# Transposing queries and keys in 32x32 blocks on VectorE instead of TensorE, in a fused attention and expert-layer kernel

## The chip, the cores and the metric

The kernel runs on one core of a Trainium2 chip. The metric is the device time of one execution in microseconds (us). In the profile the engines are PE (TensorE matmul), PEld (TensorE weight load), DVE (VectorE), ACT (ScalarE), POOL (GpSimd) and SP (SyncE, which issues DMAs); "L412" is line 412 of the kernel file.

## The reference

Attention over 8 batches, 8 heads, 576 positions and a head width of 64, causal by blocks of 64 positions; then a layer with a softmax-gated activation and a normalization on the 4608 tokens.

```python
scores = scale * np.matmul(q, k.transpose(0, 1, 3, 2))       # scale = 1/8
scores = np.where(block_i >= block_j, scores, -1e9)          # blocks of 64
attn = np.exp(scores - max); attn = attn / (sum + 1e-09)
x = np.matmul(attn, v)            # heads side by side: x is [4608, 512]

h = x @ w_in                      # w_in [512, 1024]
sm = softmax(h); solu = h * sm
ln = (solu - mean) / np.sqrt(var + 1e-06) * g_ln
out = ln @ w_out                  # w_out [1024, 512]
```

q, k and v come as float32; w_in, w_out and g_ln are drawn with float64 words, and the kernel turns the weights' 64-bit words into float32 on the chip.

## The kernel before

**Work units.** There are 32 pairs (a batch and two of its heads) of attention and 36 tiles of 128 tokens for the expert layer ("moe" in the code). Four pairs give one batch of 576 tokens. The attention output of a batch stands in `xt`, which has three buffers; the third is also scratch space for preparing the weights (line 329), so the attention of batch 2 cannot write it before the weights are ready.

**Precision by two words.** Products that need more than TensorE's fast fp32r form are split: a value is converted to a high part and the low part is the difference (`qh`, `ql`, `kh`, `kl`, the weights' `wih`, `wil`, `woh`, `wol`, and the tiles' `xh`, `xl`, `ch`, `cl`). Three matmuls make one product: high x high, low x high, high x low.

**One pair, before** (lines 386 to 546). SP loads queries and keys with the positions on the partitions: `qr` holds four blocks of 128 positions, both heads side by side; `kr` holds the four blocks of keys and a fifth block, with the last 64 keys in its upper half and the last 64 queries in its lower half (lines 391 to 408). The runs in memory are 64 floats, 256 bytes. TensorE transposes the nine blocks against an identity matrix into PSUM (`trans`, lines 410 to 412, called at 419 and 420). ScalarE converts the PSUM results to the high parts (helper `copy`, line 384), VectorE subtracts for the low parts (L424, L425), and two small copies (ScalarE) and two small subtractions (VectorE, L429) put the last 64 queries of the two heads into the block-diagonal tiles `qdh` and `qdl`. The score matmuls (L445, and L439 for the last block) read these. Then come masks (L464), row maxima (L468, VectorE), exponentials (L472, ScalarE), reciprocals (L480, L481), the scaling of the probabilities (L488 on GpSimd, or L489 on VectorE), transposes of the probabilities (L499), and the product with v (L532). Queries' and keys' split tiles have two buffers, by even and odd pairs; `qr` and `kr` have one each.

**One tile of the expert layer** (lines 549 to 643). High and low parts of x (L564 or L572, L568), 24 matmuls with w_in (L589), maximum, exponential, product, centring, square, eight transposes (L624), their split (L628, L629), 24 matmuls with w_out (L637), the scaled copy to `ob` (L641) and the store (L643).

**Preparing the weights** (`prep`, lines 333 to 355, 16 pieces of 128x512). SP loads the raw words (L337) into `ub`; ScalarE turns the low words into integers (L339); VectorE clamps the high words (L340); a scaling down runs on ScalarE, GpSimd or VectorE (L341 to L343); VectorE shifts and joins (L344, L345) and adds the low words (L346); the pieces of w_out are multiplied by g (L349 ScalarE or L350 VectorE); the high part is converted (L351 or L352) and the low part subtracted (L353 VectorE or L354 GpSimd).

**What sets the order.** Every step is an `Op` with an engine, a planned duration in ns, a key, and the buffers that it reads and writes. `Schedule.run` (lines 101 to 192) simulates the five engines with these durations when the kernel is built: when an engine is free, it takes the ready operation with the smallest key, TensorE only if PSUM slots are free, and VectorE's operations that are marked `port` never in the same planned time as an operation of GpSimd. The order that comes out is the order of the instructions on the chip; the chip's own times are then ruled by semaphores. The keys are the pair's number, or `NP + h0 + done * hs` for tile `done`, plus a number for each kind of step out of `PARAMS`. An operation may have alternatives on other engines, with a penalty that is added to its key; an alternative with a penalty of 3 or more is not admitted (line 71). Names that end in "32" are for the first four pairs. `SWITCH` is the planned cost when TensorE goes over to another kind of operand layout (`mode`).

**PSUM.** Two slots of two banks ("D") and four of one bank ("S"). Before the change the transposed keys take a D slot and the transposed queries an S slot.

Of the kernel before, what the change touches and what calls it, by code (L numbers as in the profile page):

```python
# [195 lines left out]
def kernel(  # L196
# [136 lines left out]
    def prep(i, src, hi, lo, gcol, name, key):  # L333
# [6 lines left out]
        op("DVE", 335, lambda: DVE.tensor_scalar(out=T2, in0=high, scalar1=TOP, scalar2=-TOP, op0=ALU.min, op1=ALU.max), r=[kr_], w=[k2], key=key, port=True)  # L340
# [46 lines left out]
    def attention(p):  # L387
# [5 lines left out]
        for nm, src, dst, dk in (("qr", q, qr, K["ld" + sfx]), ("kr", k, kr, K["ld" + sfx]), (f"vr{i}", v, vt, K["lv" + sfx])):  # L393

            def load(nm=nm[:2], src=src, dst=dst, dma=ACT if p == 0 and nm == "kr" else SP):
                for h in range(2):
                    dma.dma_start(
                        dst[:, 0:4, 64 * h : 64 * h + 64],
                        src[b0, 2 * hp + h, 0:512, :].rearrange("(c p) d -> p c d", p=P),
                    )  # L400
# [7 lines left out]
            op("SP", {"qr": 1460, "kr": 1820, "vr": 1640}[nm[:2]], load, w=[nm], key=(K["l0"] if p == 0 else p) + dk, tail=2100)

        def trans(src, ps, n_):  # L410
            for c in range(n_):
                PE.transpose(PS(ps)[:, c * P : (c + 1) * P], src[:, c, :], ident)  # L412


        pq, pk = newps("S"), newps("D")
# [7 lines left out]
        copy(0, 512, lambda: (qh_, PS(pq)[:, 0:512]), 0.125, [("qh", i)], ke, pq)
        op("DVE", t_dve(S), lambda: DVE.tensor_tensor(out=kl_, in0=PS(pk)[:, 0:S], in1=kh_.bitcast(F32), op=ALU.subtract), r=[("kh", i)], w=[("kl", i)], key=ke, ps=pk)  # L424
        op("DVE", t_dve(512), lambda: DVE.scalar_tensor_tensor(out=ql_, in0=PS(pq)[:, 0:512], scalar=0.125, in1=qh_.bitcast(F32), op0=ALU.mult, op1=ALU.subtract), r=[("qh", i)], w=[("ql", i)], key=ke, ps=pq)  # L425
        for h in range(2):
            own, c_ = half[h], slice(64 * h, 64 * h + 64)
            copy(0, 64, lambda own=own, c_=c_: (qdh_[own, c_], PS(pk)[own, S : S + 64]), 0.125, [("qdh", i, h)], ke, pk)
            op("DVE", t_dve(64), lambda own=own, c_=c_: DVE.scalar_tensor_tensor(out=qdl_[own, c_], in0=PS(pk)[own, S : S + 64], scalar=0.125, in1=qdh_[own, c_].bitcast(F32), op0=ALU.mult, op1=ALU.subtract), r=[("qdh", i, h)], w=[("qdl", i, h)], key=ke, ps=pk)  # L429
# [258 lines left out]
```

## Time and profile before

| | |
|---|---|
| median of 3 runs | 811.03 us (810.62 to 813.65) |
| the profiled execution | 810.45 us, its span 808.7 us |
| mean granted TensorE clock | 0.985 |
| transposes of keys, queries on TensorE (L412) | 160 and 128 instructions |
| DMA | 123798 packets, 47.06 MB; 117072 packets under 512 bytes |
| loads of q, k and v | 128 KB: median 2.4 to 2.6 us from issue to landing; 32 KB: 2.2 to 2.4 us |
| loads of weights | 512 KB: 4.2 us (w_in), 3.5 us (w_out) |

A row of a group gives line, engine, operation, output <- inputs, shapes and count, then the busy time in us and the mean of one in ns, then the engine's idle time just before these instructions and what ended it. A row of the timeline gives start and length in us and how many instructions in a row were merged. TensorE's matmuls are pipelined, their ends are modelled, and a matmul's length overlaps with the next; from start to start is what it holds the engine.

### The profile page before, as it was taken

The page shows a single profiled execution, that of the slowest core. Times are in us where ns is not written, and L with a number is a line of the kernel's source. Part 1 is how long each engine was busy: PE and PEld are TensorE (multiplying, and loading weights), DVE is VectorE, ACT ScalarE, POOL GpSimd, SP SyncE. Part 2 cuts the span into 40 slices and gives each one's busy share as a digit, 9 for nine tenths or more (in the row PEclk, how much of TensorE's full clock was granted, in tenths as well). Part 3 has the DMA queues.
Part 4 walks back from the last instruction along what each step waited for, and adds up shares of the span by engine and source line. Part 5 has one row for each costly group of instructions (what it writes and reads, how often), then busy time and mean ns, then how long its engine had stood idle before and what let it go on. Part 6 is the DMA issues. An engine that isn't in the chain of part 4 may idle for free.

```text
span 808.7 us, 14263 instructions
## 1 busy us (share of the span) xinstructions
PE 785.2 (97%) x4975; PEld 623.2 (77%) x4975; DVE 464.5 (57%) x1248; ACT 536.5 (66%) x1414; POOL 238.4 (29%) x407
## 2 busy tenths in 40 slices
PE   7788899999999999999999999999999999999998
PEld 6656678777887877777878877777778787788886
DVE  4999997555455655544555455555445554344352
ACT  5998887667566766767766676776676666433243
POOL 2323643242323332223333333222333334011100
PEclk8989999999999999999999999999999999999999
DMA  7546421112221221122212222112221100000011
GB/s 168 150 119 165 128 62 30 51 45 59 58 58 45 58 58 45 42 57 58 58 44 58 45 58 58 43 50 51 58 58 51 50 19 12 27 22 18 13 40 39
DMA packets 123798, 47.06 MB, mean 58 GB/s; under 512 B 117072, under 2 KB 117072, under 8 KB 123728
## 3 DMA queue, kind: packets, MB, share of 16 engines
q1 hardware_dynamic: 122672, 45.90, 21.7%
q8 instruction: 39, 0.64, 0.3%
q10 hardware_dynamic: 1056, 0.26, 0.2%
q14 instruction: 31, 0.25, 0.1%
HBM read 36.70 MB, written 9.44 MB: 57 GB/s over the span
## 4 chain that ended last, share of the span: by engine, by line
PE 86%; ACT 5%; DVE 5%; issue 2%; POOL 1%; SPq 1%; DMA 1%; DVEq 0%; POOLq 0%
PE ps L589 25%; PE ps L637 23%; PE ps L499 10%; PE ps L532 9%; PE ps L445 8%; PE ps L624 5%; PE ps L412 3%; PE ps L439 3%; ACT pb L472 2%; DVE nm L468 1%; ACT xt L384 1%; POOL pb L488 1%; ACT pt L384 1%; DMA ub<-in_moe_w_in_dram 1%; PE ps L281 0%
## 5 line engine op out<-in xcount | busy, mean ns | idle before, releaser
L488 POOL TENSOR_SCALAR pb<-pb,rz 128x512 f32<-128x512 f32 (+4 forms) x267 | 150.7, 585 | 241.0 <-DVE rz L481 203.7
L472 ACT ACTIVATE pb<-ps,nm 128x384 f32<-128x384 f32 (+4 forms) x288 | 155.5, 548 | 68.7 <-DVE nm L468 68.6
L468 DVE TENSOR_REDUCE nm<-ps 128x1 f32<-128x384 f32 (+4 forms) x288 | 132.1, 505 | 53.3 <-PE ps L439 53.0
L384 ACT ACTIVATE pt<-ps 128x512 f32<-128x512 f32 (+1 forms) x224 | 113.6, 556 | 48.5 <-PE ps L499 47.6
L499 PE MATMUL ps<-ident,pb 128*128 128x128 f32 x800 | 111.0, 281 | 10.1 <-ACT pb L472 7.3
L499 PEld LDWEIGHTS ps<-ident,pb 128*128 128x128 f32 x800 | 93.2, 144 | 24.8 <-ACT pb L472 8.9
L612 POOL TENSOR_TENSOR ms<-ms,mhalf 128x1 f32<-128x1 f32 x36 | 19.9, 554 | 261.2 <-DVE ms L609 261.2
L532 PE MATMUL ps<-pt,vr 128*64 128x320 f32 (+4 forms) x896 | 93.6, 360 | 0.0
L629 DVE TENSOR_TENSOR cl<-ps,ch 128x512 fp32r<-128x512 f32 x72 | 47.7, 687 | 75.1 <-ACT ch L628 74.6
L589 PE MATMUL ps<-wih,xh 128*128 128x512 f32 x288 | 85.0, 417 | 0.0
L532 PEld LDWEIGHTS ps<-pt,vr 128*64 128x64 f32 x896 | 59.5, 137 | 32.9 <-issue 0.7
L637 PE MATMUL ps<-woh,ch 128*128 128x512 f32 x288 | 84.0, 413 | 0.0
L589 PE MATMUL ps<-wil,xh 128*128 128x512 f32 x288 | 78.9, 396 | 0.0
L637 PE MATMUL ps<-wol,ch 128*128 128x512 f32 x288 | 78.9, 395 | 0.0
L637 PE MATMUL ps<-woh,cl 128*128 128x512 f32 x288 | 78.6, 394 | 0.0
L589 PE MATMUL ps<-wih,xl 128*128 128x512 f32 x288 | 78.3, 393 | 0.0
L598 DVE TENSOR_SCALAR ms<-ms 128x1 f32<-128x1 f32 x36 | 5.5, 153 | 108.2 <-ACT ob L641 108.2
L641 ACT ACTIVATE ob<-ps,ms 128x512 f32<-128x512 f32 x36 | 24.8, 688 | 60.0 <-PE ps L637 55.1
L589 PEld LDWEIGHTS ps<-wil,xh 128*128 128x128 f32 x288 | 54.3, 188 | 12.8
L637 PEld LDWEIGHTS ps<-wol,ch 128*128 128x128 f32 x288 | 54.2, 188 | 12.8
L637 PEld LDWEIGHTS ps<-woh,cl 128*128 128x128 f32 x288 | 54.1, 188 | 12.9
L589 PEld LDWEIGHTS ps<-wih,xl 128*128 128x128 f32 x288 | 54.1, 188 | 12.6
(82 smaller groups left out, 1302.0 us busy)
## 6 DMA issues: line engine op xcount, KB each, us to landing
out_dram<-ob SPq DMA_DIRECT2D x36, 256.0 KB, 2.0
qr<-in_q_dram SPq DMA_DIRECT2D x64, 128.0 KB, 2.5
vr<-in_v_dram SPq DMA_DIRECT2D x64, 128.0 KB, 2.4
kr<-in_k_dram SPq DMA_DIRECT2D x62, 128.0 KB, 2.6
ub<-in_moe_w_in_dram SPq DMA_DIRECT2D x8, 512.0 KB, 4.2
ub<-in_moe_w_out_dram SPq DMA_DIRECT2D x8, 512.0 KB, 3.5
kr<-in_k_dram SPq DMA_DIRECT2D x32, 32.0 KB, 2.3
kr<-in_q_dram SPq DMA_DIRECT2D x32, 32.0 KB, 2.2
```

Source lines behind the costliest of these rows:

```text
L384: op("ACT", t_act(n_), lambda: ACT.activation(aps()[0], aps()[1], AF.Copy, scale=scale), r=r, w=w, key=key, ps=ps, alts=[("DVE", t_dve(n_) ...
L445: PE.matmul(PS(sps[h])[:, off : off + 128 * (i_ + 1)], w_[half[h], 128 * i_ : 128 * i_ + 128], x_[half[h], 0 : 128 * (i_ + 1)], start=n_ = ...
L468: op("DVE", t_dve(wid[u]), lambda sp=sp, off=off, u=u: DVE.tensor_reduce(out=nm_[u], in_=PS(sp)[:, off : off + wid[u]], axis=AX.X, op=ALU. ...
L472: op("ACT", t_act(wid[u], 186), lambda sp=sp, off=off, u=u, zg=zg, zc=zc: ACT.activation(pb[:, poff[u] : poff[u] + wid[u]], PS(sp)[:, off ...
L488: op("POOL", 0.836 * nn + 243, lambda b=b, nn=nn, zg=zg, zc=zc: POOL.tensor_scalar(out=pb[:, poff[b] : poff[b] + nn], in0=pb[:, poff[b] : ...
L499: PE.transpose(t[:, (s_ - c0) * P : (s_ - c0 + 1) * P], pb[:, poff[b] + j * P : poff[b] + (j + 1) * P], ident)
L532: PE.matmul(PS(avs[ph])[half[h], 64 * o_ : 64 * (o_ + n_)], vt[:, j, 64 * h : 64 * h + 64], pt_.rearrange("p s q -> p (s q)")[:, 128 * s_ ...
L589: PE.matmul(o_, a_[:, c, :], w_[:, c, s_], start=(si == 0 and c == 0), stop=(si == 2 and c == NKI - 1))
L624: PE.transpose(t_[:, c * P : (c + 1) * P], u[:, (4 * hf + c) * P : (4 * hf + c + 1) * P], ident)
L629: op("DVE", t_dve(512), lambda cs=cs, cps=cps: DVE.tensor_tensor(out=cl[:, cs, :].rearrange("p c q -> p (c q)"), in0=PS(cps), in1=ch[:, cs ...
L637: PE.matmul(o_, a_[:, c, :], w_[:, c, :], start=(hf == 0 and si == 0 and c == 0), stop=(hf == 1 and si == 2 and c == 7))
L641: op("ACT", t_act(512, 93), lambda: ACT.activation(ob[i], PS(ops_)[:, 0:DM], AF.Copy, scale=m[:, 3:4]), r=[("m3", i)], w=[("ob", i)], key= ...
```

## The change

**Loads.** Instead of `qr` and `kr`, each pair loads `qz` and `kz` [128, 576]. Four DMAs for each: DMA g fills partitions 32g to 32g + 31 with head g // 2 and columns 32 (g % 2) to 32 (g % 2) + 31 of its 64, as 18 blocks of 32 positions side by side. The runs in memory are 32 floats, 128 bytes. For the first pair the keys' four DMAs are issued by ScalarE's queue, all others by SP. The loads of v stay.

**Transposes.** VectorE transposes each 32x32 block of `kz` and `qz` within its place (two instructions of 128x576), which gives `kt` and `qt`: head and column on the partitions, position along the row, in SBUF. TensorE's transposes and their two PSUM slots are gone.

**Splits.** ScalarE, or GpSimd by an alternative, converts `kt` and `qt` to the high parts; VectorE subtracts for the low parts, now from SBUF. The keys' subtraction may also go to GpSimd if its penalty is admitted (a_kl is 129.132, so it is not). Queries are split over all 576 positions, and the last 64 go into `qdh` and `qdl` by four small copies on GpSimd; the two copies and two subtractions from PSUM are gone.

**Weights.** The clamp, the low words and the g scale get GpSimd as an alternative (the penalty of the low words, a_t3, is 111.852, so that one is not admitted; those of the clamp, -246.845, and of the g scale, -26.262, are).

**The plan.** `SWITCH` goes from 130 to 165; a planned 120 ns (`SLACK`) is added before a PSUM slot counts as free; the planned length of 12 matmuls goes from 12 x 231.5 to 12 x 233 ns; and all numbers in `PARAMS` are others, so the order of the whole program is planned anew.

```diff
-SWITCH = 130.0
+SWITCH = 165.0
+SLACK = 120.0
...
-    "nd": 2, "ld": 18.299, "lv": 3.426, "q": 15.658, "qe": 164.691, "s": -4.256, "se": -95.989,
+    "nd": 2, "ld": -112.86, "lv": 9.571, "q": 88.586, "qe": 132.144, "s": 58.329, "se": -84.684,
...
-    "h0": 143.478, "hs": 1.593, "h": -14.76, "he": 13.349, "c": 136.065, "sq": -88.891, "ct": -107.468,
+    "h0": 193.882, "hs": 32.26, "h": 3.059, "he": 101.927, "c": 19.936, "sq": -24.214, "ct": -56.228,
...
-    "e1": 248.397, "e2": 84.748, "a_sp": 15.65, "a_sp32": -32.586, "a_lf": -56.56, "a_w": 0.642,
+    "e1": 312.118, "e2": 188.943, "a_sp": 284.421, "a_sp32": 90.642, "a_lf": -193.984, "a_w": -185.932,
...
-                            heapq.heappush(events, (t + LAT[o.eng]["PE"], n, 3, x, None))
+                            heapq.heappush(events, (t + LAT[o.eng]["PE"] + SLACK, n, 3, x, None))
...
-    qr = sb("qr", [4, P])
-    kr = sb("kr", [5, P])
+    qz, kz, qt, kt = (sb(x, [S]) for x in ("qz", "kz", "qt", "kt"))
...
-        op("DVE", 335, lambda: DVE.tensor_scalar(out=T2, in0=high, scalar1=TOP, scalar2=-TOP, op0=ALU.min, op1=ALU.max), r=[kr_], w=[k2], key=key, port=True)
+        op("DVE", 335, lambda: DVE.tensor_scalar(out=T2, in0=high, scalar1=TOP, scalar2=-TOP, op0=ALU.min, op1=ALU.max), r=[kr_], w=[k2], key=key, port=True,
+           alts=[("POOL", 640, lambda: POOL.tensor_scalar(out=T2, in0=high, scalar1=TOP, scalar2=-TOP, op0=ALU.min, op1=ALU.max), K["a_cm"])])
...
+        for nm, src, dst in (("kz", k, kz), ("qz", q, qz)):
+
+            def load(nm=nm, src=src, dst=dst):
+                for g in range(4):
+                    dma = ACT if p == 0 and nm == "kz" else SP
                     dma.dma_start(
-                        dst[:, 0:4, 64 * h : 64 * h + 64],
-                        src[b0, 2 * hp + h, 0:512, :].rearrange("(c p) d -> p c d", p=P),
+                        dst[32 * g : 32 * g + 32, :].rearrange("p (g d) -> p g d", d=32),
+                        src[b0, 2 * hp + g // 2, :, 32 * (g % 2) : 32 * (g % 2) + 32].rearrange("(g p) d -> p g d", p=32),
                     )
...
-        op("PE", 109 * 5, lambda: trans(kr, pk, 5), r=["kr"], w=["k2"], key=kk, opens=pk)
-        op("PE", 109 * 4, lambda: trans(qr, pq, 4), r=["qr"], w=["q2"], key=kk, opens=pq)
...
+            op("DVE", t_dve(S), lambda z=z, t=t: DVE.transpose(t, z), r=[x + "z"], w=[x + "t"], key=kk)
+            op("ACT", t_act(S), lambda t=t, hi=hi, scale=scale: ACT.activation(hi, t, AF.Copy, scale=scale), r=[x + "t"], w=[(x + "h", i)], key=ke,
+               alts=[("POOL", 0.836 * S + 243, lambda t=t, hi=hi, scale=scale: POOL.tensor_scalar(out=hi, in0=t, scalar1=scale, scalar2=1.0, op0=ALU.mult, op1=ALU.mult), K["a_qh"])])
...
+                op("DVE", t_dve(S), lambda: DVE.tensor_tensor(out=kl_, in0=kt, in1=kh_.bitcast(F32), op=ALU.subtract), r=["kt", ("kh", i)], w=[("kl", i)], key=ke, port=True,
...
+        for x, dst, src in (("qh", qdh_, qh_), ("ql", qdl_, ql_)):
+            op("POOL", 300, lambda dst=dst, src=src: last(dst, src), r=[(x, i)], w=[(x + "d", i)], key=ke)
```

More of the change, by code (lines that the diff above doesn't have):

```diff
@@ L338, in prep @@
         high = raw[:, :, 1].bitcast(F32)
-        op("ACT", 520, lambda: ACT.activation(T3.bitcast(I32), raw[:, :, 0], AF.Copy, scale=2.0**-29), r=[kr_], w=[k3], key=key)
-        op("DVE", 335, lambda: DVE.tensor_scalar(out=T2, in0=high, scalar1=TOP, scalar2=-TOP, op0=ALU.min, op1=ALU.max), r=[kr_], w=[k2], key=key, port=True)
+        op("ACT", 520, lambda: ACT.activation(T3.bitcast(I32), raw[:, :, 0], AF.Copy, scale=2.0**-29), r=[kr_], w=[k3], key=key,
+           alts=[("POOL", 640, lambda: POOL.tensor_scalar(out=T3.bitcast(I32), in0=raw[:, :, 0], scalar1=2.0**-29, scalar2=1.0, op0=ALU.mult, op1=ALU.mult), K["a_t3"])])
+        op("DVE", 335, lambda: DVE.tensor_scalar(out=T2, in0=high, scalar1=TOP, scalar2=-TOP, op0=ALU.min, op1=ALU.max), r=[kr_], w=[k2], key=key, port=True,
+           alts=[("POOL", 640, lambda: POOL.tensor_scalar(out=T2, in0=high, scalar1=TOP, scalar2=-TOP, op0=ALU.min, op1=ALU.max), K["a_cm"])])
         op("ACT", 520, lambda: ACT.activation(T2, T2, AF.Copy, scale=DOWN), r=[k2], w=[k2], key=key,
@@ L392, in attention @@
         nm_, z_, rz_ = nmt[i], zt[i], rzt[i]
-        for nm, src, dst, dk in (("qr", q, qr, K["ld" + sfx]), ("kr", k, kr, K["ld" + sfx]), (f"vr{i}", v, vt, K["lv" + sfx])):
-            def load(nm=nm[:2], src=src, dst=dst, dma=ACT if p == 0 and nm == "kr" else SP):
-                for h in range(2):
+        half = [slice(0, 64), slice(64, 128)]
+        for nm, src, dst in (("kz", k, kz), ("qz", q, qz)):
+            def load(nm=nm, src=src, dst=dst):
+                for g in range(4):
+                    dma = ACT if p == 0 and nm == "kz" else SP
@@ L408, in attention @@
[L408 to L415, printed above, removed]
+                        dst[32 * g : 32 * g + 32, :].rearrange("p (g d) -> p g d", d=32),
+                        src[b0, 2 * hp + g // 2, :, 32 * (g % 2) : 32 * (g % 2) + 32].rearrange("(g p) d -> p g d", p=32),
+                    )
@@ new lines, in attention, with loadv @@
+            op("SP", 1600, load, w=[nm], key=(K["l0"] if p == 0 else p) + K["ld" + sfx], tail=2400)
+        def loadv():
+            for h in range(2):
+                SP.dma_start(
+                    vt[:, 0:4, 64 * h : 64 * h + 64],
+                    v[b0, 2 * hp + h, 0:512, :].rearrange("(c p) d -> p c d", p=P),
+                )
+            SP.dma_start(
+                vt[0:64, 4, :].rearrange("p (h d) -> p h d", h=2),
+                v[b0, 2 * hp : 2 * hp + 2, 512:576, :].rearrange("h p d -> p h d"),
+            )
@@ L423, in attention @@
[L423 to L429, printed above, removed]
+        for x, z, t, hi, lo, scale in (("k", kz, kt, kh_, kl_, 1.0), ("q", qz, qt, qh_, ql_, 0.125)):
+            op("DVE", t_dve(S), lambda z=z, t=t: DVE.transpose(t, z), r=[x + "z"], w=[x + "t"], key=kk)
+            op("ACT", t_act(S), lambda t=t, hi=hi, scale=scale: ACT.activation(hi, t, AF.Copy, scale=scale), r=[x + "t"], w=[(x + "h", i)], key=ke,
+               alts=[("POOL", 0.836 * S + 243, lambda t=t, hi=hi, scale=scale: POOL.tensor_scalar(out=hi, in0=t, scalar1=scale, scalar2=1.0, op0=ALU.mult, op1=ALU.mult), K["a_qh"])])
+            if x == "q":
+                op("DVE", t_dve(S), lambda: DVE.scalar_tensor_tensor(out=ql_, in0=qt, scalar=0.125, in1=qh_.bitcast(F32), op0=ALU.mult, op1=ALU.subtract), r=["qt", ("qh", i)], w=[("ql", i)], key=ke, port=True)
+            else:
+                op("DVE", t_dve(S), lambda: DVE.tensor_tensor(out=kl_, in0=kt, in1=kh_.bitcast(F32), op=ALU.subtract), r=["kt", ("kh", i)], w=[("kl", i)], key=ke, port=True,
+                   alts=[("POOL", 1380, lambda: POOL.tensor_tensor(out=kl_, in0=kt, in1=kh_.bitcast(F32), op=ALU.subtract), K["a_kl"])])
@@ L431, in attention, with last @@
+        def last(dst, src):
+            for h in range(2):
+                POOL.tensor_copy(dst[half[h], 64 * h : 64 * h + 64], src[half[h], 512:576].bitcast(F32))
+        for x, dst, src in (("qh", qdh_, qh_), ("ql", qdl_, ql_)):
+            op("POOL", 300, lambda dst=dst, src=src: last(dst, src), r=[(x, i)], w=[(x + "d", i)], key=ke)
         for g, (kind, us, masks) in enumerate(groups):
@@ L448, in attention @@
                 d, md = 3 * (t_mm(320) + t_mm(256)), 0
-                rd = [(x, i) for x in ("kh", "kl")] + [(x, i, h) for h in range(2) for x in ("qdh", "qdl")]
+                rd = [(x, i) for x in ("kh", "kl", "qhd", "qld")]
                 tiles = [(sps[0], [(LAST, 192)])]
@@ L454, in attention @@
                 tiles = [(sps[h], [((h, i_), off) for i_, off in us]) for h in range(2)]
-            op("PE", d, scores, r=rd + ["q2", "k2"], w=[("P2", i, u) for _, t in tiles for u, _ in t], key=p + K["s" + sfx], opens=tuple(sps), mode=md)
+            op("PE", d, scores, r=rd, w=[("P2", i, u) for _, t in tiles for u, _ in t], key=p + K["s" + sfx], opens=tuple(sps), mode=md)
             for sp, us_ in tiles:
```

23 lines of the change are left out of this document (9 added, 14 removed), and 8 rows, old and new, of the table PARAMS.

## Prediction

> **What bounds the kernel now.** I read first the page's busy shares and the chain that ended last, then a table of stages, then the order of TensorE's work in one steady cycle.
>
> ```profile
> span 808.7 us, 14263 instructions
> PE 785.2 (97%) x4975; PEld 623.2 (77%) x4975; DVE 464.5 (57%) x1248; ACT 536.5 (66%) x1414; POOL 238.4 (29%) x407
> PE ps L589 25%; PE ps L637 23%; PE ps L499 10%; PE ps L532 9%; PE ps L445 8%; PE ps L624 5%; PE ps L412 3%; PE ps L439 3%; ACT pb L472 2%; DVE nm L468 1%; ACT xt L384 1%; POOL pb L488 1%; ACT pt L384 1%; DMA ub<-in_moe_w_in_dram 1%; PE ps L281 0%
> ```
>
> TensorE is busy 97% of the span, and the transposes that the change removes (L412) are 3% of the chain. The stages, with busy time of PE, PEld, DVE, ACT and POOL, the granted clock, the DMA share and GB/s:
>
> ```profile
> 0.00:20.00 20.00, 15.58 (x82) 12.36 (x83) 9.65 (x31) 10.82 (x31) 5.08 (x24) 0.82 0.71 169
> 20.00:110.00 90.00, 77.11 (x527) 59.05 (x527) 87.24 (x226) 79.52 (x221) 33.16 (x37) 0.91 0.48 133
> 110.00:130.00 20.00, 18.69 (x132) 14.57 (x130) 16.94 (x42) 17.48 (x42) 11.71 (x17) 1.00 0.20 46
> 130.00:700.00 570.00, 568.94 (x3751) 451.94 (x3750) 306.76 (x858) 389.37 (x1053) 174.92 (x305) 1.00 0.19 49
> 700.00:809.00 109.00, 104.85 (x492) 85.26 (x490) 43.89 (x94) 39.29 (x70) 13.53 (x26) 1.00 0.07 27
> ```
>
> There are two regimes. From 130 us on TensorE is the bound: 568.94 of 570 us busy, VectorE 54%, ScalarE 68%. From 20 to 110 us, where the weights are prepared beside the first pairs, VectorE is the bound: 87.24 of 90 us (97%), ScalarE 88%, and TensorE has gaps and a clock of 0.91. Before 130 us TensorE lacks 130 - (15.58 + 77.11 + 18.69) = 18.6 us; afterwards 1.1 and 4.2 us. So the same removed instruction is worth its full time after 130 us and nothing by itself before.
>
> **What a removed transpose is worth.** Starts on TensorE in a steady cycle, and the transposes that begin between 100 and 700 us:
>
> ```profile
> 297.17 0.71 PE L412 MATMUL ps<-ident,kr 128*128 128x128 f32 x5
> 297.71 0.60 PE L412 MATMUL ps<-ident,qr 128*128 128x128 f32 x4
> 298.07 1.18 PE L637 MATMUL ps<-woh,ch 128*128 128x512 f32 x4
> ...
> 319.50 0.71 PE L412 MATMUL ps<-ident,kr 128*128 128x128 f32 x5
> ...
> L412 PE MATMUL ps<-ident,kr x125: 271/272/332, 116.0 to 655.7; 128*128 128x128 f32 x125
> ```
>
> The means of the instructions overlap, so I go by starts: nine transposes hold the engine from 297.17 to 298.07, 0.90 us, in a cycle of 22.33 us (297.17 to 319.50). What follows, L637, starts at once, so 0.90 us is what the cycle loses. 125 / 5 = 25 pairs transpose after 100 us, the first of them at 116; 24 lie in the TensorE-bound stage. Term one: 24 x 0.90 = **-21.6 us**. The other 8 pairs' 7.2 us lie in the stage that VectorE binds and only turn into idle time.
>
> What takes over after the removal: in 130:700, per pair of 23.75 us, ScalarE works 16.2 us and VectorE 12.8 us. VectorE gets about 1.1 us more (below), ScalarE a little less; both fit in a cycle of 21.4 us. The new chain load, VectorE transpose, conversion, subtraction is longer than the old one, but the operands have two buffers and no longer need PSUM, so it can run a pair ahead. I take it as hidden there by the 21 us of other work per pair; without that cover it would cost its two transposes and two subtractions, some 3 us a pair by the rows below.
>
> **What VectorE gains and loses in the first 130 us.**
>
> ```profile
> L468 DVE TENSOR_REDUCE nm<-ps 128x1 f32<-128x576 f32 x32 | 24.0, 750 | 53.1 <-PE ps L439 53.0
> L424 DVE TENSOR_TENSOR kl<-ps,kh 128x576 fp32r<-128x576 f32 x32 | 24.1, 754 | 8.5 <-ACT kh L384 7.8 <-ACT qdh L384 0.7
> L425 DVE SCALAR_TENSOR_TENSOR ql<-ps,qh 128x512 fp32r<-128x512 f32 x32 | 21.8, 681 | 6.8 <-ACT qh L384 6.8
> L429 DVE SCALAR_TENSOR_TENSOR qdl<-ps,qdh 64x64 fp32r<-64x64 f32 x64 | 14.1, 220 | 0.6
> L384 ACT ACTIVATE qdh<-ps 64x64 fp32r<-64x64 f32 x64 | 13.9, 217 | 7.5 <-DVE kl L424 7.0
> L352 DVE CAST woh<-xt 128x512 fp32r<-128x512 f32 x3 | 1.2, 412 | 0.0
> L568 POOL TENSOR_TENSOR xl<-xt,xh 128x512 fp32r<-128x512 f32 x32 | 41.2, 1287 | 21.6 <-PE ps L589 20.3 <-DVE xh L572 1.3
> L340 DVE TENSOR_SCALAR xt<-ub 128x512 f32<-128x512 f32 x16 | 6.8, 426 | 0.0
> L489 DVE TENSOR_SCALAR pb<-pb,rz 128x384 f32<-128x384 f32 (+4 forms) x21 | 7.5, 416 | 0.1
> L488 POOL TENSOR_SCALAR pb<-pb,rz 128x512 f32<-128x512 f32 x61 | 43.4, 724 | 18.2 <-DVE rz L481 9.0 <-ACT kh L384 3.1 <-ACT pt L384 2.9
> ```
>
> No VectorE transpose is in this trace. Its bounds for 128x576 fp32: as fast as the cast, 0.412 x 576/512 = 0.46 us, or as slow as GpSimd's two-input pass, 1.287 x 576/512 = 1.45 us. I take 0.75 us, as the two 128x576 rows that pass one element after the other (0.750 and 0.754). Per pair: two transposes +1.50; queries' low part over 576 columns instead of 512 +0.09; the two small subtractions for the last block (L429) -0.44. Net +1.15 us, for 8 pairs **+9.2 us**. Out go the weights' clamp, 16 x 0.426 = 6.8 us, if the planner gives it to GpSimd, and the 7.5 us of softmax scaling on VectorE (L489): the penalty a_sp32 goes from -32.6 to 90.6, and an alternative is only admitted under 3, so these 21 go to GpSimd for certain. VectorE's account: 9.2 - 14.3 = **-5.1 us**. With a transpose of 0.46 us it is -9.7; with 1.45 us +6.1; with no clamp moved +1.7.
>
> GpSimd had 38 of the first 110 us busy (5.08 + 33.16). It gains at 0.72 us each (the 128x512 row) 16 clamps and 21 scalings, 27 us, and the small copies for the last block: about 65 of 110, so it is not the bound. ScalarE loses two 0.22 us copies a pair and can hand the g scale over; it does not bind later than VectorE.
>
> The GpSimd work has another price, the way VectorE and GpSimd get at SBUF:
>
> ```profile
> 78.83 1.27 POOL L568 TENSOR_TENSOR xl<-xt,xh 128x512 fp32r<-128x512 f32 x1
> 78.84 0.68 DVE L425 SCALAR_TENSOR_TENSOR ql<-ps,qh 128x512 fp32r<-128x512 f32 x1
> 79.44 0.69 DVE L480 TENSOR_SCALAR z<-z 128x3 f32<-128x3 f32 x1
> ...
> L480 DVE TENSOR_SCALAR z<-z x64: 153/172/991, 15.0 to 679.0; 128x6 f32<-128x6 f32 x32, 128x3 f32<-128x3 f32 x32
> ```
>
> While GpSimd's pass ran until 80.10, the subtraction that reads PSUM kept its usual 0.68 us, but the small SBUF-only operation took 0.69 us instead of 0.17 (median) and ended as GpSimd did. After the change both subtractions read SBUF alone. In the first 130 us that is 16 operations; with GpSimd busy 37% (33.16 of 90) and a wait of half a 0.72 us operation, 16 x 0.37 x 0.36 = **+2 us**. In the TensorE-bound stage the same waits lie under TensorE's work.
>
> **The loads.** Rows of 256 bytes become 128 bytes for queries and keys: 2304 packets a pair become 4608. In 130:700 the 16 DMA engines were busy 0.19 x 16 x 570 / 24 = 72 us per pair; put wholly on the 3456 small packets of q, k and v that is at most 21 ns each. If a half-size packet costs as much, a pair's queries and keys take 4608 x 21 / 16 = 6.0 us instead of 3.0. In the steady stage the DMA share goes from 0.19 to about 0.33; nothing waits. Between 0 and 110 us it goes from 0.52 to about 0.74; the loads there are asked for a pair ahead, so I cost that at nothing. Only the very first pair has no cover: at most +3.0 us, at least 0; I take **+2 us**, since the keys' chain can start while the queries still arrive. The SP queue gets 11 issues a pair instead of 9, about 0.5 us each in 21 us:
>
> ```profile
> L397 SPq DMA_DIRECT2D qr<-in_q_dram x36: 497/518/817, 209.0 to 591.8; - x36
> ```
>
> The Trainium skill, page "DMA: Bandwidth & Descriptors", section "Why small descriptors are slow (HBM only)", gives each packet a fixed three cycles beside one cycle per 32 bytes. By it, as an estimate, a 128-byte packet costs 7 cycles against 11, the first pair loses 0.8 us instead of 3.0, and the sum below is some 1 us lower. No run here has such packets yet.
>
> **The sum.** First 130 us: -5.1 + 2 + 2 = -1.1 us. Against the profiled execution: 810.45 (1.75 of it outside the span) - 21.6 - 1.1 = 787.8 us; the median of the runs, 811.03, lies 0.6 above the profiled one, so 788.
>
> **Rivals.** First the forecast itself, 788: its own range is 780 to 794, from the transpose at 0.46 us (783) to no clamp moved (794).
>
> *GpSimd blocks VectorE in the weights' stage.* Five operations of each of the 16 weight pieces and the 16 subtractions, 96 in all, use SBUF alone on VectorE. If GpSimd's share there rises from 0.37 to 0.60, 80 x 0.23 x 0.36 + 16 x 0.60 x 0.36 = 10 us are lost instead of 2: 796, and 802 with a slower transpose. For it: the 79.44 row. Against it: the plan already keeps such operations apart. The Trainium skill says this as a rule, page "SBUF — State Buffer", section "SBUF: two separate sides": VectorE and GpSimd share one pair of ports, held for a whole instruction, also by a VectorE operation with two SBUF inputs. The 79.44 row agrees.
>
> *The gaps of the first stage fill.* More freedom for the weights' steps takes VectorE and ScalarE off the end of that stage, and of TensorE's 18.6 us of gaps before 130 us only some 6 stay: 788 - 12.6 = 775.
>
> *Attention runs ahead of the expert tiles* (the slower side). The tiles' key rises by 32.26 per tile instead of 1.593, while a pair's rises by 1. What attention alone and tiles alone cost:
>
> ```profile
> 29.80 0.77 PE L412 MATMUL ps<-ident,kr 128*128 128x128 f32 x5
> ...
> 43.78 0.77 PE L412 MATMUL ps<-ident,kr 128*128 128x128 f32 x5
> ...
> 702.10 11.16 PE ps L589 x48
> 726.16 11.16 PE ps L589 x48
> ```
>
> A pair with no tile beside it takes 13.98 us (29.80 to 43.78); a tile alone 12.03 us (two in 702.10 to 726.16). Together 26.0 us against 22.33 mixed: each pair that comes apart loses 3.7 us and its 0.90 us gain. Five such pairs eat the 22.7 us; twelve of 24 give 788 + 12 x 4.6 = 843. Against it: the attention output has three buffers, so attention cannot lead far, and TensorE takes any ready work.
>
> *The cycle does not shorten.* Another engine turns out to hold the 22.33 us, and only the small first-stage terms change: about 809. Against it: 99.8% TensorE with ScalarE at 68%.
>
> **Chances and range.** Forecast 0.66, blocked ports 0.15, filled gaps 0.10, attention ahead 0.05, cycle unchanged 0.04. One measurement of this kernel tells about 0.5% (4 us) from no change, so below 807 is faster: 0.66 + 0.15 + 0.10 = 0.91; within 0.5%: 0.04; slower: 0.05. The range 775 to 800 takes in the filled gaps and most of the blocked ports and leaves out the last two.
>
> **What would show it.** L412 gone; the steady cycle near 21.4 us with TensorE still above 99% busy from about 130 us; VectorE transposes near 0.75 us; the weights' clamp and all softmax scaling on GpSimd; TensorE's lack before 130 us near 25 us, since its removed work turns into idle time there. Wrong would be: a steady TensorE share under 97%, a transpose over 1.5 us, VectorE operations stretched beside GpSimd, or weights ready later than the last prepared piece is now.

## The result and the profile after

| | before | after |
|---|---|---|
| median | 812.34 us (4 runs, 810.62 to 814.20) | 790.44 us (4 runs, 788.92 to 791.23) |
| ratio, 95% interval | | 0.9728 (0.9697 to 0.9758) |
| profiled execution, its span | 810.45 us, 808.7 us | 790.35 us, 788.6 us |
| TensorE busy, and the rest of the span | 785.2 us, 23.5 us | 760.3 us, 28.3 us |

The forecast was 788 us in a range of 775 to 800. The page after, first its head, then its busy shares and the chain that ended last:

```profile
span 788.6 us, 13834 instructions
PE 760.3 (96%) x4687; PEld 595.4 (76%) x4687; DVE 471.7 (60%) x1191; ACT 521.6 (66%) x1349; POOL 341.7 (43%) x593
PE ps L650 25%; PE ps L602 25%; PE ps L512 10%; PE ps L545 9%; PE ps L458 8%; PE ps L637 4%; PE ps L452 3%; ACT pb L485 2%; DVE nm L481 1%; DMA ub<-in_moe_w_out_dram 1%; DMA kz<-in_k_dram 1%; DMA ub<-in_moe_w_in_dram 1%; POOL pb L501 0%; ACT xt L389 0%; DVE ql L432 0%
```

TensorE has 288 instructions less, and its transposes of queries and keys, 3% of the chain before, have no successor there. GpSimd went from 238.4 to 341.7 us. (Lines have moved: scores are L458 and L452 now, the transposes of probabilities L512, the product with v L545, the expert matmuls L602 and L650.) The stages after, with the same columns as before (PE, PEld, DVE, ACT, POOL, clock, DMA share, GB/s):

```profile
0.00:20.00 20.00, 9.70 (x46) 7.66 (x46) 11.78 (x30) 10.59 (x27) 8.57 (x29) 0.81 0.91 184
20.00:110.00 90.00, 78.31 (x522) 58.74 (x524) 81.97 (x200) 77.58 (x216) 62.77 (x99) 0.85 0.62 130
110.00:130.00 20.00, 18.03 (x129) 13.17 (x123) 18.10 (x45) 16.55 (x45) 12.42 (x20) 1.00 0.48 113
130.00:700.00 570.00, 569.52 (x3602) 447.31 (x3603) 325.42 (x847) 384.83 (x1013) 247.54 (x431) 1.00 0.22 47
700.00:789.00 89.00, 84.75 (x395) 68.53 (x393) 34.39 (x72) 32.06 (x54) 10.39 (x18) 0.99 0.07 27
```

The two regimes stand as before: TensorE 99.9% busy from 130 to 700 us, and a first stage in which it has gaps, now 130 - (9.70 + 78.31 + 18.03) = 24.0 us against 18.6. The steady cycle in TensorE's order of time, one matmul group and the same group a cycle later:

```profile
299.20 1.10 PE L602 MATMUL ps<-wil,xh 128*128 128x512 f32 x4
...
320.65 1.10 PE L602 MATMUL ps<-wil,xh 128*128 128x512 f32 x4
```

21.45 us against 22.33: 0.88 us less per pair. What the new operations cost, in the groups of VectorE and GpSimd:

```profile
L434 DVE TENSOR_TENSOR kl<-kt,kh 128x576 fp32r<-128x576 f32 x32 | 25.9, 809 | 1.3 <-ACT kh L429 1.3
L432 DVE SCALAR_TENSOR_TENSOR ql<-qt,qh 128x576 fp32r<-128x576 f32 x32 | 25.7, 803 | 0.1
L428 DVE STREAM_TRANSPOSE kt<-kz 128x576 f32<-128x576 f32 x32 | 24.8, 775 | 6.6 <-DMA kz<-in_k_dram 6.5
L428 DVE STREAM_TRANSPOSE qt<-qz 128x576 f32<-128x576 f32 x32 | 24.5, 766 | 1.1 <-DMA qz<-in_q_dram 0.8
L343 DVE TENSOR_SCALAR xt<-ub 128x512 f32<-128x512 f32 x9 | 3.8, 419 | 0.3 <-DMA ub<-in_moe_w_out_dram 0.3
...
L501 POOL TENSOR_SCALAR pb<-pb,rz 128x384 f32<-128x384 f32 (+4 forms) x288 | 176.6, 629 | 241.4 <-DVE rz L494 227.2
L439 POOL CAST qdh<-qh 64x64 fp32r<-64x64 f32 x64 | 26.7, 417 | 4.3 <-ACT qh L429 2.1
L439 POOL CAST qdl<-ql 64x64 fp32r<-64x64 f32 x64 | 17.4, 273 | 6.3 <-DVE ql L432 4.2
L344 POOL TENSOR_SCALAR xt<-ub 128x512 f32<-128x512 f32 x7 | 5.2, 739 | 3.2 <-DVE xt L349 1.9 <-DMA ub<-in_moe_w_in_dram 0.9
```

A transpose takes 0.77 us, all 288 softmax scalings run on GpSimd, and 7 of the 16 clamps do (L344); 9 stayed on VectorE (L343).

### The profile page after: what moved, and what is told of

It reads as the page before. It is cut to its first block, busy times and chain, and to the rows that moved or that the text cites. A ratio compares the mean times of both kernels' runs of the same rounds, so it can differ in the third digit from the quotient of the medians.

```text
span 788.6 us, 13834 instructions
## 1 busy us (share of the span) xinstructions
PE 760.3 (96%) x4687; PEld 595.4 (76%) x4687; DVE 471.7 (60%) x1191; ACT 521.6 (66%) x1349; POOL 341.7 (43%) x593
## 3 DMA queue, kind: packets, MB, share of 16 engines
q1 hardware_dynamic: 196112, 45.87, 26.9%
## 4 chain that ended last, share of the span: by engine, by line
PE 86%; ACT 5%; DVE 4%; DMA 2%; issue 1%; POOL 1%; SPq 0%; DVEq 0%; ACTq 0%; POOLq 0%
PE ps L650 25%; PE ps L602 25%; PE ps L512 10%; PE ps L545 9%; PE ps L458 8%; PE ps L637 4%; PE ps L452 3%; ACT pb L485 2%; DVE nm L481 1%; DMA ub<-in_moe_w_out_dram 1%; DMA kz<-in_k_dram 1%; DMA ub<-in_moe_w_in_dram 1%; POOL pb L501 0%; ACT xt L389 0%; DVE ql L432 0%
## 5 line engine op out<-in xcount | busy, mean ns | idle before, releaser
L501 POOL TENSOR_SCALAR pb<-pb,rz 128x384 f32<-128x384 f32 (+4 forms) x288 | 176.6, 629 | 241.4 <-DVE rz L494 227.2
L485 ACT ACTIVATE pb<-ps,nm 128x256 f32<-128x256 f32 (+4 forms) x288 | 155.1, 548 | 47.3 <-DVE nm L481 46.6
L389 ACT ACTIVATE pt<-ps 128x512 f32<-128x512 f32 (+1 forms) x224 | 108.5, 562 | 42.0 <-PE ps L512 41.6
L642 DVE TENSOR_TENSOR cl<-ps,ch 128x512 fp32r<-128x512 f32 x72 | 49.4, 686 | 142.7 <-ACT ch L641 142.7
L481 DVE TENSOR_REDUCE nm<-ps 128x1 f32<-128x256 f32 (+4 forms) x288 | 131.4, 509 | 2.1 <-PE ps L452 2.1
L512 PE MATMUL ps<-ident,pb 128*128 128x128 f32 x800 | 111.2, 287 | 11.2 <-POOL pb L501 6.3
L512 PEld LDWEIGHTS ps<-ident,pb 128*128 128x128 f32 x800 | 93.9, 146 | 24.6 <-POOL pb L501 9.7
L545 PE MATMUL ps<-pt,vr 128*64 128x320 f32 (+4 forms) x896 | 93.8, 360 | 0.3 <-ACT pt L389 0.3
L545 PEld LDWEIGHTS ps<-pt,vr 128*64 128x64 f32 x896 | 59.3, 137 | 34.4 <-issue 1.3
L602 PE MATMUL ps<-wih,xh 128*128 128x512 f32 x288 | 84.7, 416 | 0.2 <-ACT pb L485 0.2
L650 PE MATMUL ps<-woh,ch 128*128 128x512 f32 x288 | 83.4, 411 | 0.0
L602 PE MATMUL ps<-wil,xh 128*128 128x512 f32 x288 | 79.8, 399 | 0.0
L650 PE MATMUL ps<-wol,ch 128*128 128x512 f32 x288 | 79.0, 396 | 0.0
L602 PE MATMUL ps<-wih,xl 128*128 128x512 f32 x288 | 78.8, 395 | 0.0
L650 PE MATMUL ps<-woh,cl 128*128 128x512 f32 x288 | 78.6, 394 | 0.0
L641 ACT ACTIVATE ch<-ps 128x512 fp32r<-128x512 f32 x72 | 44.0, 611 | 49.5 <-PE ps L637 49.5
L458 PE MATMUL ps<-kh,qh 64*128 64x256 f32 (+3 forms) x256 | 57.4, 395 | 10.5 <-POOL qh L430 5.4
L602 PEld LDWEIGHTS ps<-wil,xh 128*128 128x128 f32 x288 | 54.9, 190 | 13.0
L602 PEld LDWEIGHTS ps<-wih,xl 128*128 128x128 f32 x288 | 54.4, 189 | 12.9
L650 PEld LDWEIGHTS ps<-wol,ch 128*128 128x128 f32 x288 | 54.3, 188 | 12.8
```

Source lines behind the costliest of these rows:

```text
L389: op("ACT", t_act(n_), lambda: ACT.activation(aps()[0], aps()[1], AF.Copy, scale=scale), r=r, w=w, key=key, ps=ps, alts=[("DVE", t_dve(n_) ...
L458: PE.matmul(PS(sps[h])[:, off : off + 128 * (i_ + 1)], w_[half[h], 128 * i_ : 128 * i_ + 128], x_[half[h], 0 : 128 * (i_ + 1)], start=n_ = ...
L481: op("DVE", t_dve(wid[u]), lambda sp=sp, off=off, u=u: DVE.tensor_reduce(out=nm_[u], in_=PS(sp)[:, off : off + wid[u]], axis=AX.X, op=ALU. ...
L485: op("ACT", t_act(wid[u], 186), lambda sp=sp, off=off, u=u, zg=zg, zc=zc: ACT.activation(pb[:, poff[u] : poff[u] + wid[u]], PS(sp)[:, off ...
L501: op("POOL", 0.836 * nn + 243, lambda b=b, nn=nn, zg=zg, zc=zc: POOL.tensor_scalar(out=pb[:, poff[b] : poff[b] + nn], in0=pb[:, poff[b] : ...
L512: PE.transpose(t[:, (s_ - c0) * P : (s_ - c0 + 1) * P], pb[:, poff[b] + j * P : poff[b] + (j + 1) * P], ident)
```

## The experiments

The theory: the gain is TensorE's own time in the stage that it binds, and the first stage, which VectorE binds, gives nothing and takes little. The rivals: the new plan makes the gain; the small packets, the first pair's late start or GpSimd's part hold the first stage. Twelve kernels; each was timed beside the kernel before, which gave 811.06 to 812.43 us in these sessions. Where only an emitted instruction was changed, the order of all others stayed that of the changed kernel; where a number of the plan was changed, the whole order was planned anew.

| kernel | median, us | ratio to before, 95% interval | TensorE idle in the first 160 us |
|---|---|---|---|
| changed | 790.44 | 0.9728 (0.9697 to 0.9758) | 24.4 |
| old_path_new_plan | 837.40 | 1.0290 (1.0259 to 1.0322) | 20.4 |
| nine_back_late | 811.02 | 0.9987 (0.9976 to 0.9999) | 25.8 |
| nine_back_early | 790.23 | 0.9726 (0.9710 to 0.9743) | 19.6 |
| long_runs | 789.92 | 0.9726 (0.9706 to 0.9746) | 25.8 |
| dve_twice_early | 802.70 | 0.9898 (0.9876 to 0.9921) | 34.8 |
| dve_twice_late | 793.52 | 0.9783 (0.9767 to 0.9798) | 26.2 |
| one_block_early | 785.97 | 0.9684 (0.9654 to 0.9715) | 22.0 |
| keys_on_sp | 789.92 | 0.9734 (0.9719 to 0.9749) | 24.7 |
| weights_not_on_pool | 800.19 | 0.9863 (0.9838 to 0.9888) | 35.2 |
| scaling_on_dve | 793.51 | 0.9779 (0.9763 to 0.9794) | 27.0 |
| first1_tensor | 788.43 | 0.9722 (0.9695 to 0.9749) | 22.9 |
| first4_tensor | 792.67 | 0.9769 (0.9743 to 0.9794) | 19.3 |

The last column is 160 us less TensorE's busy time in that window; in the kernel before it is 18.6. It is good to some 1.5 us only: nine_back_late, whose first ten pairs are those of the changed kernel, has 25.8 for 24.4. The granted TensorE clock of the first 130 us differs between these profiles too (0.87 in the changed kernel's, 0.96 in keys_on_sp's), and the times of those two executions are the same, 790.35 and 789.89 us.

**Where a transpose on TensorE costs time.** Nine transposes of the identity, put back ahead of a pair's first scores, for the late or for the early pairs:

```diff
+                if g == 0 and p >= 10:        # the other kernel: p < 10
+                    for _ in range(9):
+                        PE.transpose(PS(sps[0])[:, 0:P], ident, ident)
```

> The changed kernel in its order, with nine dummy transposes of the identity on TensorE ahead of the first scores of the pairs 10 to 31, those that start after 130 us. My theory: they cost their whole time, 22 x 0.90 = 20 us, so 810 us (807 to 814), and the steady cycle is 22.3 us again. Rival (TensorE has slack in the changed kernel, another engine holds the cycle): 790 to 798 us.

Measured: 811.02 us, 20.6 us more than the changed kernel, 0.94 us for each of the 22 pairs; the whole gain is gone (0.9987). The cycle of that kernel on TensorE, and its main stage:

```profile
299.85 1.14 PE L457 MATMUL ps<-ident 128*128 128x128 f32 x9
...
322.32 1.15 PE L457 MATMUL ps<-ident 128*128 128x128 f32 x9
...
130.00:700.00 570.00, 569.82 (x3700) 452.03 (x3701) 316.82 (x827) 378.17 (x997) 244.03 (x423) 1.00 0.22 47
```

22.47 us from one pair's dummies to the next's, 1.02 above the changed kernel's cycle. TensorE had no slack for them.

> The same nine dummy transposes, for the pairs 0 to 9 alone, which lie in the stage that prepares the weights. My theory: TensorE has gaps there, so of 10 x 0.90 = 9 us at most a third is seen: 790 to 793 us. It may even be a little faster, since busy matmuls keep the granted clock up. Rival (TensorE binds there too): 799 us.

Measured: 790.23 us, no difference. TensorE's extra work left its gaps smaller, 19.6 us in the first 160 instead of 24.4:

```profile
0.00:160.00 160.00, 140.35 (x990) 109.15 (x992) 137.37 (x332) 130.89 (x357) 105.05 (x179) 0.91 0.58 122
```

The same nine instructions cost 0.94 us a pair after 130 us, and before that nothing that these runs could tell. That is the theory's main claim.

**Whether the plan makes the gain.** The kernel before, with the changed kernel's numbers:

```diff
-SWITCH = 130.0
+SWITCH = 165.0
+SLACK = 120.0
...
-    "nd": 2, "ld": 18.299, "lv": 3.426, "q": 15.658, "qe": 164.691, "s": -4.256, "se": -95.989,
+    "nd": 2, "ld": -112.86, "lv": 9.571, "q": 88.586, "qe": 132.144, "s": 58.329, "se": -84.684,
...
```

> This is the kernel before with only the plan's numbers of the changed kernel (PARAMS, SWITCH, SLACK, 12 x 233); queries and keys are still transposed by TensorE. My theory (the gain is TensorE's 0.90 us per pair in the TensorE-bound stage): no gain, 808 to 816 us, steady cycle 22.3 us. Rival (the new plan makes the gain): 795 us or less.

Measured: 837.40 us, 25 us slower than before, outside both expectations. Its page and its main stages:

```profile
PE 800.1 (96%) x4975; PEld 630.6 (75%) x4975; DVE 462.5 (55%) x1221; ACT 536.2 (64%) x1411; POOL 270.9 (32%) x437
...
160.00:700.00 540.00, 528.89 (x3450) 415.94 (x3450) 281.85 (x783) 363.11 (x989) 176.62 (x298) 0.99 0.20 49
```

The same 4975 TensorE instructions were busy 14.9 us longer than before (the mean granted clock was 0.969, before it was 0.985), and the idle rest grew by 11.7 us; between 160 and 700 us TensorE was idle for 11.1 us, before it was 1.1. So these numbers bring no gain of their own: with the transposes on TensorE they give a worse order. nine_back_late says the same from the other side, since it keeps the new order and has no gain left. What the changed kernel would do in an order from the old numbers was not tried.

**What holds the first stage: VectorE.** Each transpose made twice for the first ten pairs, and in another kernel for the others:

```diff
-            op("DVE", t_dve(S), lambda z=z, t=t: DVE.transpose(t, z), r=[x + "z"], w=[x + "t"], key=kk)
+            op("DVE", t_dve(S), lambda z=z, t=t: [DVE.transpose(t, z) for _ in range(2 if p < 10 else 1)], r=[x + "z"], w=[x + "t"], key=kk)
```

> The changed kernel in its order, but VectorE makes each transpose twice for the pairs 0 to 9: 20 more transposes of 0.77 us, 15 us, all in the first 130 us. My theory (VectorE, 91% busy there, holds the stage in which the weights are prepared): 8 to 13 us slower, 799 to 803 us. Rival (no single engine holds it, the waits between engines do): under 5 us, 791 to 795 us.

Measured: 802.70 us, 12.3 us more, 80% of the 15.4 us that were added. TensorE's idle time before 160 us grew by 10.4 us:

```profile
20.00:110.00 90.00, 68.33 (x453) 50.58 (x454) 87.55 (x199) 70.73 (x199) 57.67 (x95) 0.82 0.59 124
```

VectorE is at 97% there and every other engine is less busy than in the changed kernel, as it must be if they wait for it.

> The changed kernel in its order, with each VectorE transpose made twice for the pairs 10 to 31, 34 us more work on VectorE, all beside a TensorE that is never idle. My theory: no change, 789 to 792 us, though the same extra work on the first ten pairs cost 12 of 15 us. Rival (the longer chain from the load to the scores reaches TensorE): 795 us or more.

Measured: 793.52 us, 3.1 us more and outside what I expected, though far under the 34 us added. The cycle did not change, and TensorE's idle time up to 700 us lies almost wholly before 200 us (0.1 us after it):

```profile
301.50 1.10 PE L602 MATMUL ps<-wil,xh 128*128 128x512 f32 x4
...
322.97 1.10 PE L602 MATMUL ps<-wil,xh 128*128 128x512 f32 x4
...
130.00:160.00 30.00, 28.54 (x198) 22.28 (x198) 26.25 (x63) 25.59 (x74) 20.19 (x34) 1.00 0.34 61
160.00:700.00 540.00, 538.55 (x3392) 420.95 (x3392) 330.77 (x826) 359.27 (x939) 228.66 (x397) 1.00 0.22 47
```

322.97 - 301.50 = 21.47 us. The line between the stages was drawn too early: in the changed kernel the last weight is finished after 157 us (below), so the next pairs still meet a busy VectorE, 88% from 130 to 160 us here. TensorE was idle for 1.5 us in that stretch and for 1.4 us more up to 200 us; in the changed kernel it was 0.5 and nothing. After that, twice the transposes cost nothing.

The opposite: for the first ten pairs VectorE transposes one block of 32 columns only, the rest of the tiles being a constant.

```diff
+    DVE.memset(kt, 0.3)
+    DVE.memset(qt, 0.3)
...
-            ... DVE.transpose(t, z) ...
+            ... DVE.transpose(t, z) if p >= 10 else DVE.transpose(t[:, 0:32], z[:, 0:32]) ...
```

> The changed kernel in its order, but for the pairs 0 to 9 VectorE transposes only the first 32 of 576 columns; the rest of the transposed tiles holds a constant set at the start while VectorE is idle, so these pairs are computed on wrong queries and keys. It gives back nearly all of the transposes' 15 us on VectorE in the first 130 us. My theory (VectorE holds that stage, and doubling cost 12 us): 6 to 12 us faster than the changed kernel, 778 to 784 us; less than the doubling cost, since the other engines come to the limit. Rival (the stage is held by the waits in the order, so relief does not pay): 787 us or more.

Measured: 785.97 us, 4.5 us less, between the two expectations, and the interval (0.9654 to 0.9715) overlaps that of the changed kernel. A transpose of 32 columns still takes 0.20 us, so 20 x (0.77 - 0.20) = 11.3 us were taken away. Adding 15 us to VectorE costs 12; taking away 11 returns some 4. This fits a VectorE that, at the changed kernel's load, is only just the last of several engines:

```profile
20.00:110.00 90.00, 79.41 (x540) 59.34 (x540) 78.47 (x204) 78.23 (x218) 65.94 (x104) 0.92 0.64 133
```

Relieved, VectorE and ScalarE stand at 87% each. What ended TensorE's waits in the changed kernel was spread as well: GpSimd's scaling of the probabilities 6.3 us, its conversion of the first pair's queries 5.4, ScalarE's exponentials 6.8. So VectorE holds the first stage in the sense that more work on it is paid for to 80%; it is not the only engine near its limit.

**The loads.** Queries and keys in runs of 2304 bytes:

```diff
-                        dst[32 * g : 32 * g + 32, :].rearrange("p (g d) -> p g d", d=32),
-                        src[b0, 2 * hp + g // 2, :, 32 * (g % 2) : 32 * (g % 2) + 32].rearrange("(g p) d -> p g d", p=32),
+                        dst[32 * g : 32 * g + 32, :],
+                        src[b0, 2 * hp + g // 2].rearrange("s d -> (s d)")[18432 * (g % 2) : 18432 * (g % 2) + 18432].rearrange("(p f) -> p f", p=32),
```

> The changed kernel in its order, but queries and keys are loaded in runs of 2304 bytes instead of 128, the same bytes in another arrangement, so the attention is computed on permuted queries and keys. It prices the small packets. My theory: the first pair starts about 2 us earlier, nothing else moves: 787 to 789 us. Rival (the DMA engines, 91% busy in the first 20 us, hold the weights' stage): 784 us or less, with the first tile of the expert layer over 4 us earlier.

Measured: 789.92 us, no difference to the changed kernel (I had expected 787 to 789); the DMA share from 130 to 700 us fell from 0.22 to 0.17. The small packets cost nothing at the end. The first pair did the reverse of what I expected. The start of the changed kernel, then of this one:

```profile
0.72 2.01 SPq L404 DMA_DIRECT2D qz<-in_q_dram  x4
1.24 1.61 ACTq L404 DMA_DIRECT2D kz<-in_k_dram  x3
3.74 0.83 SPq L339 DMA_DIRECT2D ub<-in_moe_w_in_dram  x2
6.71 0.78 DVE L428 STREAM_TRANSPOSE kt<-kz 128x576 f32<-128x576 f32 x1 [5.87 <-DMA kz<-in_k_dram]
```

```profile
2.55 0.90 SPq L339 DMA_DIRECT2D ub<-in_moe_w_in_dram  x2
3.35 0.32 ACTq L404 DMA_DIRECT2D kz<-in_k_dram  x1
8.98 0.78 DVE L428 STREAM_TRANSPOSE kt<-kz 128x576 f32<-128x576 f32 x1 [8.13 <-DMA kz<-in_k_dram]
```

SP was through with the queries sooner and issued the weights at 2.55 us, ahead of ScalarE's last DMA of keys at 3.35 us. That one landed only after the 1 MB of weights, and the first transpose started 2.3 us later than with the small packets.

> The changed kernel in its order, with the first pair's keys issued by SP ahead of its queries, instead of by ScalarE beside them, so that the weights' loads are issued 2 us later and queue behind both. My theory: the keys land about 2 us earlier than 6.7 us, the weights 2 us later, and the end does not move by more than 2 us: 788 to 792 us. Rival (the first pair's late start, 3 us, is paid at the end): 786 to 788 us.

```diff
-                    dma = ACT if p == 0 and nm == "kz" else SP
+                    dma = SP
```

Measured: 789.92 us, no difference, though the keys' transpose started at 4.85 us instead of 6.71 and the first scores at 8.75 instead of 10.60:

```profile
2.77 2.12 SPq L404 DMA_DIRECT2D qz<-in_q_dram  x4
4.85 0.78 DVE L428 STREAM_TRANSPOSE kt<-kz 128x576 f32<-128x576 f32 x1 [4.00 <-DMA kz<-in_k_dram]
4.94 0.97 SPq L339 DMA_DIRECT2D ub<-in_moe_w_in_dram  x2
8.75 0.69 PE L458 MATMUL ps<-kh,qh 64*128 64x384 f32 x2 [3.59 <-POOL qh L430]
```

From 12.86 (long runs) over 10.60 to 8.75 us, the first scores' time does not reach the end: the weights' steps fill VectorE meanwhile.

**What moved to GpSimd.** The weights' steps kept off it (a_cm at 246.845 and a_cg at 26.262 instead of their negatives):

> The changed kernel planned anew with the clamp and the g scale of the weights kept off GpSimd (the penalties with the other sign). My theory: 7 clamps of 0.42 us go back to VectorE, about 3 us more on the engine that is nearly full: 791 to 795 us. Rival (GpSimd's work in that stage blocks VectorE at the shared SBUF access): faster, 785 to 788 us.

Measured: 800.19 us, 9.8 us more, in the direction of the theory and three times its 3 us. All 16 clamps are on VectorE again, and longer:

```profile
L343 DVE TENSOR_SCALAR xt<-ub 128x512 f32<-128x512 f32 x16 | 7.7, 499 | 0.0
```

That is 3.9 us more than in the changed kernel. The rest of the 9.8 us came with the new order, TensorE's idle time before 160 us going from 24.4 to 35.2 us; which part is the clamps' and which the order's is not settled.

Softmax scaling of the first four pairs admitted on VectorE (a_sp32 at -32.586):

> The changed kernel planned anew with VectorE admitted again for the softmax scaling of the first four pairs (a_sp32 back at -32.586), 21 operations of 0.42 us at most. My theory: up to 7.5 us go back onto VectorE in the stage that it holds, 3 to 7 us slower, 793 to 798 us. Rival (GpSimd is the one that is late there, TensorE waits for its scaling): faster, 784 to 789 us.

Measured: 793.51 us, 3.1 us more, the low end of the theory; 17 scalings went to VectorE:

```profile
L502 DVE TENSOR_SCALAR pb<-pb,rz 128x256 f32<-128x256 f32 (+4 forms) x17 | 7.1, 462 | 0.0
```

Here too the whole order is new: 11 clamps went to GpSimd instead of 7, and the 5 left on VectorE took 4.5 us. So the 3.1 us are not the scalings' alone.

**A mixed version.** The first pair, or the first four, by TensorE as before, the rest by VectorE; planned anew:

```diff
+        if p < HY:                            # HY = 1, or 4
...
+            op("PE", 109 * 5, tk, r=["kz", "kt"], w=["k2"], key=kk, opens=pk)
+            op("PE", 109 * 4, tq, r=["qz"], w=["q2"], key=kk, opens=pq)
```

> The changed kernel planned anew with the first pair alone loaded and transposed as before the change (TensorE). My theory: the first scores come 3 us earlier, at 7.5 us, VectorE has 1.1 us less, and the end comes 1 to 3 us earlier: 787 to 789 us. Rival (the first pair is not what holds the stage): 790 us, or any small shift of the new order.

> The same for the first four pairs. My theory: VectorE is spared 4 x 1.1 us and GpSimd the small copies, TensorE's 3.6 us fall into its gaps: 784 to 788 us. Rival (TensorE's or PSUM's share in that stage is already the limit): 791 us or more.

Measured: 788.43 and 792.67 us. The first is 2 us under the changed kernel, as expected, but the intervals (0.9695 to 0.9749 and 0.9697 to 0.9758) are nearly the same, so it isn't shown to be faster. The second is a miss, on the side of the rival: TensorE's idle time before 160 us did fall, from 24.4 to 19.3 us, but it had 36 transposes more to do and was idle 2 us between 160 and 700, which it had not been. Whether the four pairs or the new order did this is open.

## Why the prediction was right, point by point

**The TensorE term (-21.6 us): right.** The cycle fell by 0.88 us for 0.90, and putting the work back cost 20.6 us. The count moved: the changed kernel starts ten pairs before 130 us, not eight, so 22 pairs are left for the bound stage. By what putting the work back cost, the term is 1.0 us smaller than forecast.

**Transposes before 130 us are worth nothing: right.** nine_back_early shows it to within its interval. TensorE's idle time before 130 us was forecast near 25 us and is 24.0.

**VectorE's account (-5.1 us): not confirmed.** Its busy time between 20 and 110 us went from 87.24 to 81.97 us, 5.3 less, but the account was for the first 130 us, and there it went from 9.65 + 87.24 + 16.94 = 113.83 to 11.78 + 81.97 + 18.10 = 111.85 us, 2.0 less. That the shorter window gives nearly the forecast is chance. The transpose was sized well (0.75 for 0.77), and the scaling left as argued. But two more pairs lie in the stage, and only 7 of 16 clamps left, 7 x 0.42 = 2.9 us and not 6.8. With ten pairs and seven clamps the prediction's own prices give 11.5 - 7.5 - 2.9 = +1.1 us. What it left out went the other way: the weights' scaling down on VectorE fell from 9 operations and 5.6 us to 4 and 1.7 us, and two of the 16 pieces were not yet joined at 130 us.

**The first pair (+2 us): later, as forecast, by another way and without weight.** The first scores came at 10.60 instead of 7.45 us, 3.15 later. Before:

```profile
5.12 1.05 PE L412 MATMUL ps<-ident,qr 128*128 128x128 f32 x4
7.45 0.44 PE L445 MATMUL ps<-kh,qh 64*128 64x384 f32 x2 [0.74 <-ACT kh L384]
```

After:

```profile
8.92 0.77 DVE L428 STREAM_TRANSPOSE qt<-qz 128x576 f32<-128x576 f32 x1
10.60 0.69 PE L458 MATMUL ps<-kh,qh 64*128 64x384 f32 x2 [5.44 <-POOL qh L430]
```

From the first transpose to the first scores it was 2.33 us before and is 3.89 now (from 6.71, shown above), because VectorE makes the keys' low part ahead of the queries' transpose and the scores wait for GpSimd's conversion of the queries. So half of the 3.15 us is this chain, which the term put at nothing: it counted only the loads. And keys_on_sp and long_runs show that 2 us more or less there are not seen at the end, so by these runs the term was near 0.

The price of the packets was too high as well: the dynamic queue's share rose from 21.7% of 16 engines' 808.7 us to 26.9% of 788.6, that is by 586 us for 73440 more packets, 8 ns for each added one and not 21; the share from 130 to 700 us is 0.22 and not 0.33. The rule of the Trainium skill that was weighed there, page "DMA: Bandwidth & Descriptors", section "Why small descriptors are slow (HBM only)", gives as an estimate 7 cycles for 128 bytes against 11 for 256, so 3/11 of the old price, 6 ns, for each added packet; it was nearer than my bound.

**GpSimd against VectorE (+2 us, and the rival at 796).** GpSimd went to 62.77 of 90 us, 70%, more than the rival's 60%. By the rival's own sum that is 80 x 0.33 x 0.36 + 16 x 0.70 x 0.36 = 13.5 us lost, so about 799; it was 790. The waits were there, but shorter than half a GpSimd operation. In the first 130 us the two subtractions, now from SBUF, took 0.788 and 0.834 us on average, where their shortest took 0.718 and 0.742, about 1.5 us over nine of each; single ones came to 1.062 and 1.196. The weights' shift and join lengthened from 464 and 682 ns to 502 and 715, 16 of each, 1.1 us. By this estimate the price was near the +2 us of the sum. The two kernels that took work off GpSimd again (weights_not_on_pool, scaling_on_dve) were slower, which fits, but both had a new order.

**Weights ready later.** I named this as a sign of being wrong, and it came: the last low part of w_out was started at 128.2 us before and at 157.0 after.

```profile
L359 POOL TENSOR_TENSOR wol<-xt,woh x4: 1278/1339/1652, 103.9 to 157.0; 128x512 fp32r<-128x512 f32 x4
```

TensorE was busy for 29.52 of the 30 us from 130 to 160 us all the same, so little harm is seen; the new order has two more pairs of attention under way by 130 us, which fits but was not tested by itself. The test was badly chosen: it watched one chain and not TensorE's supply.

**The other rivals.** The cycle shortened, and TensorE was never idle between 160 and 700 us, so neither an unchanged cycle nor the losses of attention drawn apart from the tiles took place. Filled gaps did not either: 24.0 us of them are left.

The sum was 787.8 us against the profiled 790.35. The 2.6 us between them are inside the ratio's interval (0.9697 to 0.9758, 5 us wide) and are not assigned. What the prediction had right is the large term and the split into stages. That the small terms of the first stage add up to so little is in part luck: VectorE's account and the first pair were both off, in opposite directions. The forecast's own range was given as 780 to 794, though its terms reach down to 783 only.

## What to carry to other kernels

Before an instruction is taken off the busiest engine, split the span by what binds each stage: here nine transposes were worth 0.94 us a pair where TensorE was never idle and nothing where VectorE held the stage. Then price what the receiving engine pays in its own tight stage, not on average; doubling the transposes cost 80% of their time there and nothing once the weights were done. A planner's numbers need not carry over to another program: taken over into the kernel before, these cost 25 us.

## What the runs showed of the hardware

In long_runs one 72 KB DMA, issued 0.8 us behind the first of two 512 KB loads of weights and from another engine's queue, landed only after them, 5.6 us after its issue; in the changed kernel, where all of the first pair's keys were issued ahead of the weights, the slowest of the loads of keys took 4.3 us. The first transpose started 2.3 us later, although all packets were eighteen times longer. GpSimd's small copies of 64x64 have a median of 0.235 us; the mean of those into qdh is 0.42 us and the longest took 0.82. Two of them that began at 313.61 us, while VectorE's subtraction of keys ran from 313.44 for 0.83 us, took 1.05 us together; the two into qdl at 317.32, with no such operation beside them, took 0.52. And VectorE's transpose of 128x576 fp32 took the time of a plain pass, 0.77 us beside 0.75 us for the row maximum of the same shape.
